# Re-ordering copies, head moves and row transposes in the first attention layer of a four-layer block

## The chip, the core and the metric

The kernel runs on one core of one Trainium2 chip. A core has five engines with instruction streams of their own: TensorE (PE, matmuls), VectorE (DVE), ScalarE (ACT), GpSimd (POOL) and SyncE (SP, which here only issues DMAs). They meet through semaphores. The metric is the device time of one execution in microseconds (us). Before the change it is 1189.37 us, the median of three runs (1189.28 to 1192.3). The profiled execution took 1192.6 us, of which 1190.8 us lie between its first and its last instruction; all times inside the profile count from that first instruction.

## What is computed

Four residual layers, in the order A, B, A, B, on x of 2048 rows and 576 columns in bf16:

```python
x = x + _A_ref(_layernorm(x, axis=-1), A_wqkv, A_wo)
x = x + _B_ref(_layernorm(x, axis=-1), B_w_in, B_w_sp, B_b_sp, B_w_out)
...                                   # the same two once more
# _A_ref: 32 heads of 18 columns; row s attends to rows s, s-2, ..., s-14 that exist
logits = where(mask, einsum(q, kg) * scale, -1e9);  o = einsum(softmax(logits), vg) @ wo
# _B_ref: z = gelu(x @ w_in); z2 = layernorm(second half of z)
# out = (first half of z * (w_sp @ z2 + b_sp)) @ w_out
```

Only the first layer A (`li == 0` in the code) is touched by the change, and the layer B behind it is where its last edits are felt.

## The kernel before

`layer_A` writes out by hand the order of instructions on every engine: inside `manual_schedule`, each engine takes its instructions in the order of the Python calls. So the text of `layer_A` is five in-order queues. The layer has three phases.

**Front (0 to 41 us).** x comes in groups of rows, called tiles, of 128 rows: `x0` holds tiles 0 to 3, `x1` tiles 4 to 7, a spare buffer tiles 8 to 11, and a fourth load tiles 12 to 15. The weights for v, q and k come on the same SP queue between them (`load_wv`, `load_wqk`; here `D` is 576, k is loaded first, then q, then a last strip of k). For a tile i, `S_(i)` takes mean and variance on DVE, `R_` raises to the power -0.5 on POOL, `A_(i)` writes the normalised rows on DVE. They are then transposed into `xnT`, by PE for tiles 0 to 3 (`T_pe`, and a copy by ACT), by SP's transposing DMA for the others (`T_`, line 249). `PG(d, qk, cc)` projects 128 columns of q or k (block d) for 512 rows (cc) with five matmuls of 128x512 (line 402), and copies the result to a staging tile `stg`; two of these tiles, for blocks 3 and 4, are borrowed from the later weight `win2a`. Once all parts of a block of 1024 rows are staged, 18-row slices, one per head, are moved to the tile `QK` by DMAs, spread over the POOL and SP queues by the `queues` argument. `VW(t, hh)` projects v with five matmuls of 128x288 (line 379). `fill_window_rows` writes constant rows of the sliding-window mask into `QK`, half a sequence at a time, in four DVE copies of 128x4096 (line 196); the moves come after the fill of their half.

**Steps (41 to 130 us).** The attention is 38 steps, two for each 112 queries: step s does the logits of step s+1 (`L_mm`, 16 matmuls, line 437), their exponentials (`EXP`, two ACT instructions, line 446), and the product with v of step s (`PV`, 16 matmuls, line 457), which ends with two DVE instructions and, every second step, a transposing DMA into `oT` (line 469). Whatever else is due in a step stands in `table`, filled by `at(step, function)`: the remaining `PG` for rows 1024 to 2047, the `VW`, `WO` (the output projection with residual, line 494), the row norms of the result (`LN_STATS`, `LN_XN`), its store (`XST`), and `LN_T(i)`, the transposing DMA of row tile i back into `xnT` for layer B (line 249 again). `oT`'s and `LN_T`'s transposes, the stores and the loads of the residual all go out on the SP queue.

**Behind it: layer B.** `p1_main(i)` starts at about 134 us. It multiplies row tile i with the second half of `w_in` (line 791), applies gelu on ACT into one of three buffers `zp` (line 805), and takes sums; `p1_norm(i)` normalises `zp` into `Z`, in part on DVE (line 832), in part on POOL (line 834), after a power on POOL (line 822). The bias `bsp` is loaded on POOL's queue into the memory of the four `ln_xn` buffers; so that load stands behind the transposes of the last row tiles, which read these buffers, and in POOL's order it stands ahead of the first power of layer B.

Of the kernel before, what the change touches and what calls it, by code (L numbers as in the profile page):

```python
# [18 lines left out]
P = 128  # L19
D = 576  # L20
# [6 lines left out]
PADL = HALO  # L27
# [35 lines left out]
class K:  # L63
# [51 lines left out]
    def build_window_rows(self, c, R):  # L115

        nc = self.nc
        self.pat = self.consts.tile([P, 2, 272], bf16, name="win_pat")
        self.patpad = self.consts.tile([P, PADL], bf16, name="win_patpad")
        n = c.tile([P, 3], i32, name="win_n")
        g = c.tile([P, 3], i32, name="win_g")
        bits = c.tile([P, 5, 3], i32, name="win_bits")
        vf = c.tile([P, 5, 3], f32, name="win_vf")
        uu = c.tile([P, 4, 2], f32, name="win_uu")
        half = WB / 2  # L130
        nc.gpsimd.iota(n[:], pattern=[[1, 3]], base=15, channel_multiplier=1)
        nc.gpsimd.memset(R[:, 0, 0:8, :], half)
        nc.gpsimd.affine_select(out=R[:, 0, 0:8, :], in_=R[:, 0, 0:8, :], compare_op=ALU.is_ge, fill=-half,
                                base=1, pattern=[[2, 8], [-1, 16]], channel_multiplier=0)
        nc.gpsimd.memset(R[:, 1, 0:8, :], 0.0)
        for off in (2, 3):
            nc.gpsimd.affine_select(out=R[:, 1, 0:8, :], in_=R[:, 1, 0:8, :], compare_op=ALU.not_equal, fill=-1.0,
                                    base=-off, pattern=[[-2, 8], [1, 16]], channel_multiplier=0)
        nc.gpsimd.memset(R[:, 1, 7, 0:2], 1.0)
        for a, v in ((0, half), (1, 1.0)):  # L140
            row = R[:, a, 12, :].rearrange("p (f e) -> p f e", e=2)
            nc.gpsimd.memset(row[:, :, 0:1], v)
            nc.gpsimd.memset(row[:, :, 1:2], -v)
        nc.gpsimd.memset(R[:, 0, 13, :], -2.5 * WB)
        nc.gpsimd.memset(R[:, 1, 13, :], 1.0)
        one = self.dram.tile([2, MR, 256], bf16, name="win_period")
        for xb in self.xn_bufs:
            nc.gpsimd.memset(xb[:, D:640], 0.0)

        def part0():  # L150
            nc.vector.tensor_scalar(out=n[:], in0=n[:], scalar1=15, scalar2=None, op0=ALU.bitwise_and)
            nc.vector.tensor_scalar(out=g[:], in0=n[:], scalar1=1, scalar2=None, op0=ALU.logical_shift_right)
            nc.vector.tensor_tensor(out=g[:], in0=g[:], in1=n[:], op=ALU.bitwise_xor)
            for i in range(4):
                nc.vector.tensor_scalar(out=bits[:, i, :], in0=g[:], scalar1=i, scalar2=1,
                                        op0=ALU.logical_shift_right, op1=ALU.bitwise_and)
            nc.vector.tensor_scalar(out=bits[:, 4, :], in0=n[:], scalar1=1, scalar2=None, op0=ALU.bitwise_and)

        def pads():
            nc.gpsimd.memset(self.pat[:], 0.0)  # L160
            nc.gpsimd.memset(self.patpad[:], 0.0)
            for j in range(4):
                nc.gpsimd.affine_select(out=self.patpad[:], in_=self.patpad[:], compare_op=ALU.not_equal, fill=1.0,
                                        base=-32 * j - 31, pattern=[[0, PADL]], channel_multiplier=1)

        def part1(eng):
            nc.vector.tensor_scalar(out=vf[:], in0=bits[:], scalar1=-2.0, scalar2=1.0, op0=ALU.mult, op1=ALU.add)
            nc.vector.tensor_scalar_mul(out=R[:, :, 0:8, :], in0=R[:, :, 0:8, :], scalar1=vf[:, 4, 1:2])
            nc.vector.tensor_tensor(out=uu[:], in0=vf[:, 0:4, 0:2], in1=vf[:, 0:4, 1:3], op=ALU.add)
            nc.vector.tensor_scalar_mul(out=R[:, 0, 8:12, :], in0=vf[:, 0:4, 1:2].to_broadcast([P, 4, 16]), scalar1=half)  # L170
            nc.vector.tensor_scalar_mul(out=R[:, 1, 8:12, 0:2], in0=uu[:, :, 0:1].to_broadcast([P, 4, 2]), scalar1=0.5)
            nc.vector.tensor_scalar_mul(out=R[:, 1, 8:12, 2:16], in0=uu[:, :, 1:2].to_broadcast([P, 4, 14]), scalar1=0.5)
            self.dma(one[:].rearrange("a r (p f) -> p (a r) f", f=16), R[0:16].rearrange("p a r f -> p (a r) f"), eng=eng)

        def load(eng):
            for j in range(4):
                self.dma(self.pat[32 * j + DH:32 * j + 32, :, 0:256], one[:].rearrange("a r x -> r a x"), eng=eng)
        self.load_pat = load
        return part0, pads, part1

    def make_ident(self):
        nc = self.nc
# [1 line left out]
        nc.gpsimd.affine_select(out=self.ident[:], in_=self.ident[:], compare_op=ALU.not_equal, fill=1.0,  # L184
                                base=0, pattern=[[-1, P]], channel_multiplier=1)

    def fill_window_rows(self, QK, half):
        nc, n = self.nc, self.cfg.S // 2
        if half == 0:
            nc.vector.tensor_copy(out=self.pat[:, :, 256:272], in_=self.pat[:, :, 0:16])  # L190
            nc.vector.tensor_copy(out=QK[:, 0, :, 0:PADL], in_=self.pat[:, 0, None, 0:PADL].to_broadcast([P, 8, PADL]))
            nc.vector.tensor_copy(out=QK[:, 1, :, 0:PADL], in_=self.patpad[:, None, :].to_broadcast([P, 8, PADL]))
        c0 = PADL + half * n
        for g0 in (0, 4):
            for a in range(2):
                nc.vector.tensor_copy(out=QK[:, a, g0:g0 + 4, c0:c0 + n].rearrange("p g (k x) -> p g k x", x=256),
                                      in_=self.pat[:, a, None, None, PADL:PADL + 256].to_broadcast([P, 4, n // 256, 256]))

    def H_tile(self, name):
        return self.ps.tile([P, 2, 512], f32, name=name, tag="H", bufs=2)  # L200
# [82 lines left out]
        nc.vector.memset(R["wv"][64:128, 4, :], 0.0)  # L283
        nc.vector.memset(R["wo"][64:128, 4, :], 0.0)

    def load_wqk(self, eng):

        R = self.right
        for c0, n, w0 in ((D, 512, D + 64), (0, D, 0), (D + 512, 64, D)):
            self.dma(R["wqk"][:, :, w0:w0 + n], self.A_wqkv[0:512, c0:c0 + n].rearrange("(c p) n -> p c n", p=P), eng=eng)  # L290
            self.dma(R["wqk4"][:64, w0:w0 + n], self.A_wqkv[512:576, c0:c0 + n], eng=eng)

# [29 lines left out]
    def layer_A(self, li):  # L322
        nc, tc, cfg = self.nc, self.tc, self.cfg
# [190 lines left out]
            self.ln_T(tails.pop(i)["xn"], i * P, P)  # L514

        q2 = (nc.gpsimd, nc.sync, nc.gpsimd)


        if li == 0:
# [10 lines left out]
            x_load(x0[:, 1:2, :], 1, 1, nc.scalar)  # L530
            x_load(x0[:, 2:4, :], 2, 2, nc.sync)
            self.load_wv(nc.sync, 2)
            x_load(x1[:, 0:4, :], 4, 4, nc.sync)
            self.load_wqk(nc.sync)
            x_load(spare, 8, 4, nc.sync)
            exp_table()
            self.zero_right()
# [46 lines left out]
            R_(1, 1)  # L584
            A_(0)
            T_pe(0)
            S_(2)
            A_(1)
            T_pe(1)
            VW(0, 0, False)  # L590
            VW(0, 1, False)
            VW(1, 0, False)
            S_(3)
            R_(2, 2)
            rows[1]()
            setup_bufs(nc.gpsimd)
            rows[2](nc.gpsimd)
            A_(2, 3)
            T_pe(2)
            T_pe(3)  # L600
            VW(1, 1, False)
            x_load(sb.tile([P, 4, D], bf16, name="x_in3", tag="x_in", bufs=2)[:], 12, 4, nc.sync)
            S_(4, 5)
# [19 lines left out]
            order = [(d, 0) for d in range(4)] + [(d, 1) for d in range(4)] + [(4, 0), (4, 1)]  # L623
            for k_, (d, cc) in enumerate(order):
                for qk in ((1, 0) if d < 4 else (0,)):
                    PG(d, qk, cc, False, (nc.gpsimd, nc.sync) if d in (0, 4) else q2)
                if k_ == 3:
                    VW(3, 0, False)
                    VW(3, 1, False)
                if k_ == 5:  # L630
                    R_(12, 4)
                    A_(12, 13, 14, 15)
# [15 lines left out]
            nvw0, nvw = 0, 4  # L648
        for t in range(nvw0, nvw - (1 if li == 0 else 0)):
            for hh in range(2):  # L650
                VW(t, hh, li == 0)

        pieces = []

# [8 lines left out]
        def at(s, f, *a):  # L663
            table.setdefault(s, []).append((f, a))
        pgs = [(d, qk, cc) for d, cc in ((0, 2), (1, 2), (2, 2), (0, 3), (1, 3), (2, 3), (3, 2), (3, 3), (4, 2), (4, 3))
               for qk in ((1, 0) if d < 4 else (0,))]
        PG_END = 14
        pre, pgs = pgs[:6], pgs[6:]
        for k_, (d, qk, cc) in enumerate(pgs):
            at(1 + k_ if li == 0 else (k_ * PG_END) // len(pgs), PG, d, qk, cc, True)  # L670
        for t in range(nvw, NT):
            for hh in range(2):
                if li == 0 and t == nvw:
                    at(13 * hh, VW, t, hh, True)
                else:
                    at(2 * t - 2 + hh, VW, t, hh, 2 * t - 2 + hh >= PG_END and hh == 0)
        for i in range(NS):
# [6 lines left out]
            at(s + 2, LN_XN, i)  # L684
            at(s + 2, XST, i)
            if i < NS - 1:
                at(max(s + 4, 24 + (5 * i) // 4) if li == 0 else s + 4, LN_T, i)
        if li == 0:
            at(0, self.load_wo, nc.sync)
            for f in reversed(self.load_win2a(nc.gpsimd)):  # L690
                at(0, f)
# [5 lines left out]
        for k_, (d, qk, cc) in enumerate(pre):  # L697
            if k_ == (2 if li == 0 else 0):
                L_mm(0)
                EXP(0)  # L700
            PG(d, qk, cc, li > 0 or k_ < 4, q2)
            if li == 0 and k_ == 3:
                self.fill_window_rows(QK, 1)
        if li == 0:
            VW(nvw - 1, 0, False)
            VW(nvw - 1, 1, False)
# [346 lines left out]
```

The softmax here doesn't subtract the row's maximum and nothing guards it: scores larger than these inputs give would overflow.

## Time and profile before

| | us |
|---|---|
| device time, median of three | 1189.37 |
| span of the profiled execution | 1190.8 |
| PE busy | 1180.2 (99%) |
| DVE busy | 547.4 (46%) |
| ACT busy | 376.6 (32%) |
| POOL busy | 281.5 (24%) |
| first layer A, up to the last output projection | about 0 to 135 |

A PE that is busy for 99% of the span leaves 10.6 us of visible idle time. To find what an edit in layer A can be worth one looks for PE's idle stretches inside the first 160 us, and for what ended each. A row of the timeline reads: start, duration, engine (SPq is SyncE's own queue, which only issues), source line, operation, output<-input, and in brackets the engine's idle time ahead of it with what ended it. A DMA has three times: when its queue issued it, how long the issue took, and when its data landed; only the last lets a waiting instruction go on. In a table of waits the numbers are the sum in us, how often, and the longest.

### The profile page before, as it was taken

What the parts mean: (1) busy time and instruction counts of PE and PEld (TensorE: products, weight loads), DVE (VectorE), ACT (ScalarE), POOL (GpSimd) and SP (SyncE); (2) the same over time, 40 slices, a digit from 0 to 9 for tenths busy, and PEclk for the clock granted to TensorE, in tenths of its full rate; (3) what the DMA queues carried; (4) which work ended last, traced back from release to release, by engine and by line L of the source; (5) the groups of instructions that cost most, each with busy time, mean ns of one, the idle gap of its engine ahead of it and who ended that gap; (6) DMA issues with size and microseconds to landing.
All of it is one profiled execution on the core that took longest, in us unless ns stands there. A gap on an engine that the chain in (4) does not pass through costs nothing.

```text
span 1190.8 us, 20761 instructions
## 1 busy us (share of the span) xinstructions
PE 1180.2 (99%) x8554; PEld 620.6 (52%) x8554; DVE 547.4 (46%) x1206; ACT 376.6 (32%) x593; POOL 281.5 (24%) x383
## 2 busy tenths in 40 slices
PE   8999999999999999999999999999999999999998
PEld 5567544444444444457755775444444444444677
DVE  8688587333233233245556786753233233233311
ACT  5578677210110110202156786760110110111000
POOL 4768685000000000001153877530000000000000
PEclk9999999999999999999999999999999999999999
DMA  8989992000000000049645999900000000000332
GB/s 195 200 163 199 181 224 65 23 4 9 12 12 12 12 1 11 12 139 291 169 98 117 203 227 196 202 14 9 12 12 1 12 12 12 12 1 28 125 105 73
DMA packets 178104, 101.21 MB, mean 85 GB/s; under 512 B 134336, under 2 KB 159360, under 8 KB 178009
## 3 DMA queue, kind: packets, MB, share of 16 engines
q1 hardware_dynamic: 165144, 78.13, 30.6%
q0 software_dynamic: 6512, 16.00, 5.4%
q10 hardware_dynamic: 6352, 5.75, 1.6%
q8 instruction: 67, 1.10, 0.4%
q14 instruction: 29, 0.23, 0.1%
HBM read 42.39 MB, written 16.53 MB: 49 GB/s over the span
## 4 chain that ended last, share of the span: by engine, by line
PE 94%; DMA 3%; POOL 1%; ACT 0%; issue 0%; SPq 0%; DVE 0%; ACTq 0%; DVEq 0%
PE pg L887 42%; PE pz L869 12%; PE po L941 12%; PE pz L791 11%; PE pp L402 5%; PE pw L494 3%; PE O_ps L457 3%; PE pv L379 3%; PE L_ps L437 2%; DMA oT<-o_t 2%; PE pzs L791 1%; DMA QK<-win2a 1%; POOL QK L77 1%; DMA wqk_sb<-in_A_wqkv_dram 1%; ACT P_sb L446 0%
## 5 line engine op out<-in xcount | busy, mean ns | idle before, releaser
L887 PE MATMUL pg<-Wq,Z 128*128 128x512 bf16 x2304 | 502.8, 379 | 0.0
L887 PEld LDWEIGHTS <-Z 128*128 128x128 bf16 x2304 | 225.3, 98 | 272.0
L891 DVE TENSOR_TENSOR g_tmp<-pg,ln_xn 128x512 f32<-128x512 f32 x144 | 99.6, 692 | 429.2 <-PE pg L887 429.2
L881 ACT ACTIVATE z1T<-pz 128x1024 bf16<-128x1024 f32 x72 | 73.7, 1024 | 513.8 <-PE pz L869 513.6
L77 POOL DMA_DIRECT2D wout<-in_B_w_out_dram x4 | 4.3, 1064 | 604.6 <-PE pg L887 604.6
L941 PE MATMUL po<-wout,Z 128*128 128x288 bf16 x1152 | 141.4, 286 | 0.0
L446 ACT ACTIVATE P_sb<-L_ps 128x896 bf16<-128x896 f32 (+1 forms) x152 | 126.7, 887 | 41.2 <-PE L_ps L437 40.6
L869 PE MATMUL pz<-xnT,w 128*128 128x512 bf16 (+1 forms) x640 | 136.0, 380 | 0.0
L941 PEld LDWEIGHTS <-Z 128*128 128x128 bf16 x1152 | 112.7, 98 | 28.8
L791 PEld LDWEIGHTS <-xnT 128*128 128x128 bf16 (+1 forms) x800 | 66.2, 97 | 81.0 <-issue 23.7
L791 PE MATMUL pz<-win2a,xnT 128*128 128x512 bf16 x384 | 104.8, 380 | 0.0
L892 DVE TENSOR_TENSOR Z<-g_tmp,z1T 128x512 bf16<-128x512 f32 x144 | 99.6, 692 | 9.7
L869 PEld LDWEIGHTS <-w 128*128 128x128 bf16 (+1 forms) x640 | 51.1, 97 | 80.0 <-issue 27.1
L402 PE MATMUL pp<-xnT,wqk_sb 128*128 128x512 bf16 x360 | 83.8, 382 | 0.5 <-DMA wqk_sb<-in_A_wqkv_dram 0.5
L805 ACT ACTIVATE zp<-pz 128x1024 bf16<-128x1024 f32 x64 | 65.5, 1024 | 36.6 <-PE pz L791 32.8
L951 DVE TENSOR_TENSOR x_new<-po,xo 128x288 f32<-128x288 f32 (+1 forms) x64 | 28.8, 455 | 87.6 <-PE po L941 83.5
L791 PE MATMUL pz<-win2b,xnT 128*128 128x512 bf16 (+1 forms) x256 | 65.7, 380 | 0.0
L807 DVE CUSTOM_DVE_ANT_0 Z<-zp 128x1536 bf16<-128x1536 bf16 x32 | 56.6, 1769 | 13.1 <-ACT zp L805 13.0
L77 POOL DMA_DIRECT2D QK<-stg x81 | 50.7, 631 | 36.3 <-DVE stg L371 21.0
L379 PE MATMUL pv<-wv_sb,xnT 128*128 128x288 bf16 (+1 forms) x380 | 55.8, 285 | 0.0
L242 POOL TENSOR_SCALAR ln_xn<-x_new,ln_mv,ln_rstd 128x576 bf16<-128x576 f32 x23 | 52.8, 2294 | 2.0
L402 PEld LDWEIGHTS <-wqk_sb 128*128 128x128 bf16 x360 | 33.2, 98 | 37.2 <-DMA wqk_sb<-in_A_wqkv_dram 1.0
(114 smaller groups left out, 916.9 us busy)
## 6 DMA issues: line engine op xcount, KB each, us to landing
xres<-x_new SPq DMA_DIRECT2D x48, 288.0 KB
xo<-xres SPq DMA_DIRECT2D x32, 288.0 KB
wout<-in_B_w_out_dram POOLq DMA_DIRECT2D x4, 1296.0 KB, 8.5
xo<-xres SPq DMA_DIRECT2D x8, 576.0 KB
w<-in_B_w_in_dram SPq DMA_DIRECT2D x16, 256.0 KB
QK<-stg POOLq DMA_DIRECT2D x53, 72.0 KB, 4.4
QK<-stg SPq DMA_DIRECT2D x41, 72.0 KB
xo<-in_A_x_dram SPq DMA_DIRECT2D x8, 288.0 KB
```

The lines of the kernel that those rows point to most:

```text
L77: return eng.dma_start(out=out, in_=in_)
L379: nc.tensor.matmul(pv[:nk, 0:288], lhsT=self.xnT[:, c, QT * t:QT * t + nk], rhs=wv_sb[:, c, hh * 288:(hh + 1) * 288], start=(c == 0), stop ...
L402: nc.tensor.matmul(pp[:, :], lhsT=w, rhs=self.xnT[:, c, PADL + cc * 512:PADL + (cc + 1) * 512], start=(c == 0), stop=(c == 4))
L446: nc.scalar.activation(out=P_bufs[(2 * s + jp) % 4][:nk, :, :, 0:nq], in_=Lv[:nk, :, :, 0:nq], func=ACT.Exp, scale=scale)
L791: nc.tensor.matmul(pzvs[ci][:, sub * 512:sub * 512 + w], lhsT=self.xnT[r0:r1, c, PADL + i * P:PADL + (i + 1) * P], rhs=win2(c)[r0:r1, c0 + ...
L805: nc.scalar.activation(out=zp[:, c0:c0 + cn], in_=pzvs[ci][:, 0:cn], func=ACT.Gelu_apprx_tanh, accum_out=sums[:, ci:ci + 1])
L869: nc.tensor.matmul(pz1s[q // 2][:, q % 2, :], lhsT=w1[r0:r1, c, sub * P:(sub + 1) * P], rhs=self.xnT[r0:r1, c, PADL + q * 512:PADL + (q + ...
L881: nc.scalar.activation(out=z1T[:, q2 * 512:(q2 + 2) * 512], in_=pz1s[q2 // 2][:, :, :].rearrange("p a b -> p (a b)"), func=ACT.Gelu_apprx_ ...
L887: nc.tensor.matmul(pg[:, :], lhsT=Z[:, jj, i, sub * P:(sub + 1) * P], rhs=Wq[q][:, i, :], start=(i == 0), stop=(i == NS - 1))
L891: nc.vector.tensor_tensor(out=tmp[:], in0=pg[:, :], in1=bsp[:, qs], op=ALU.add)
L892: nc.vector.tensor_tensor(out=uT(jj)[:, sub, qs], in0=tmp[:], in1=z1Ts[jj, sub][:, qs], op=ALU.mult)
L941: nc.tensor.matmul(acc[hh], lhsT=uT(j // 2)[:, j % 2, i * P:(i + 1) * P], rhs=wouts[j // NJH][:, j % NJH, hh * 288:(hh + 1) * 288], start= ...
```

## The change

It has six parts, all in the first attention layer:

1. **Loads.** `load_wqk` is cut in pieces: k and the first 256 columns of q (`q0`) are now issued before x tiles 4 to 7, the rest of q (`q1`) and the last strip of k behind them.
2. **First row norms.** The small DVE instructions that build the mask pattern (`part1`, now without its store) move ahead of the norm of tile 1; the statistics of tiles 2 and 3 follow that norm, and each of these two tiles has its own power. The pattern's memsets and its store on POOL come after tile 3.
3. **Mask copies.** The fill of the second half, four copies in one go before the steps, becomes one copy at the end of each of steps 0 to 3.
4. **Last head moves.** The eight moves of block 4 of the first half go to SP seven times out of eight, where they alternated between POOL and SP.
5. **Order of projections.** `VW(9, 1)` moves from step 13 to step 1; twelve `PG` that stood one in each of steps 1 to 12 now stand two in step 2 and one in each of steps 3 to 12. `VW` of t = 4 and 5 are copied out by ACT where DVE did it.
6. **Late row transposes.** `LN_T` of row tiles 4 to 11 moves from steps 29, 30, 31, 32, 34, 35, 36, 37 to steps 34, 34, 35, 35, 36, 36, 37, 37; those of tiles 12 to 14 from steps 39, 40, 41 to steps 36, 38, 41.

The purpose is to have PE wait less for data: for q's weights, for the second step's head moves, and for the `oT` transposes at the end. Between the two programs nothing else changes: PE has the same number of instructions in both.

```diff
-        def part1(eng):
+        def part1():
...
+        def store(eng):
             self.dma(one[:].rearrange("a r (p f) -> p (a r) f", f=16), R[0:16].rearrange("p a r f -> p (a r) f"), eng=eng)
...
-    def fill_window_rows(self, QK, half):
+    def fill_window_rows(self, QK, half, parts=((0, 0), (0, 1), (4, 0), (4, 1))):
...
-    def load_wqk(self, eng):
+    def load_wqk(self, eng, names=("k", "q", "k1")):
...
-        for c0, n, w0 in ((D, 512, D + 64), (0, D, 0), (D + 512, 64, D)):
+        parts = dict(k=(D, 512, D + 64), q=(0, D, 0), q0=(0, 256, 0), q1=(256, D - 256, 256), k1=(D + 512, 64, D))
+        for c0, n, w0 in (parts[k_] for k_ in names):
...
+        q7 = (nc.sync,) * 7 + (nc.gpsimd,)
...
             self.load_wv(nc.sync, 2)
+            self.load_wqk(nc.sync, ("k", "q0"))
             x_load(x1[:, 0:4, :], 4, 4, nc.sync)
-            self.load_wqk(nc.sync)
+            self.load_wqk(nc.sync, ("q1", "k1"))
...
             A_(0)
             T_pe(0)
-            S_(2)
+            rows[2]()
             A_(1)
             T_pe(1)
+            S_(2)
+            R_(2, 1)
             VW(0, 0, False)
             VW(0, 1, False)
             VW(1, 0, False)
             S_(3)
-            R_(2, 2)
+            R_(3, 1)
+            A_(2)
+            T_pe(2)
+            A_(3)
+            T_pe(3)
             rows[1]()
             setup_bufs(nc.gpsimd)
-            rows[2](nc.gpsimd)
-            A_(2, 3)
-            T_pe(2)
-            T_pe(3)
+            rows[3](nc.gpsimd)
...
-                    PG(d, qk, cc, False, (nc.gpsimd, nc.sync) if d in (0, 4) else q2)
+                    PG(d, qk, cc, False, (nc.gpsimd, nc.sync) if d == 0 else q2 if d < 4 else q7)
...
-                VW(t, hh, li == 0)
+                VW(t, hh, li == 0 and t > 5)
...
-            at(1 + k_ if li == 0 else (k_ * PG_END) // len(pgs), PG, d, qk, cc, True)
+            at(2 + (11 * k_) // 12 if li == 0 else (k_ * PG_END) // len(pgs), PG, d, qk, cc, True)
...
-                    at(13 * hh, VW, t, hh, True)
+                    at(hh, VW, t, hh, True)
...
-                at(max(s + 4, 24 + (5 * i) // 4) if li == 0 else s + 4, LN_T, i)
+                at(s + 4 if li > 0 or i > 11 else 24 + i if i < 4 else 34 + (i - 4) // 2, LN_T, i)
...
+            for k_, part in enumerate(((0, 0), (0, 1), (4, 0), (4, 1))):
+                at(k_, self.fill_window_rows, QK, 1, (part,))
...
-            if li == 0 and k_ == 3:
-                self.fill_window_rows(QK, 1)
```

More of the change, by code (lines that the diff above doesn't have):

```diff
@@ L178, in build_window_rows @@
         self.load_pat = load
-        return part0, pads, part1
+        return part0, pads, part1, store
     def make_ident(self):
@@ L193, in fill_window_rows @@
         c0 = PADL + half * n
[L194 to L197, printed above, removed]
+        for g0, a in parts:
+            nc.vector.tensor_copy(out=QK[:, a, g0:g0 + 4, c0:c0 + n].rearrange("p g (k x) -> p g k x", x=256),
+                                  in_=self.pat[:, a, None, None, PADL:PADL + 256].to_broadcast([P, 4, n // 256, 256]))
     def H_tile(self, name):
```

## The prediction, on record before the run

> **What bounds the kernel now.** I read the page's first part, then PE's table of waits for 5 to 160 us, then the timelines of PE, DVE, POOL, ACT and SP around each wait, with the landing times that the trace's semaphore updates give.
>
> ```profile
> PE 1180.2 (99%) x8554; PEld 620.6 (52%) x8554; DVE 547.4 (46%) x1206; ACT 376.6 (32%) x593; POOL 281.5 (24%) x383
> ...
> PE pw L494 <- DMA oT<-o_t: 1.8, 2, 1.2
> PE pt L574 <- DVE ln_xn L567: 1.2, 2, 0.8
> PE L_ps L437 <- ACT P_sb L446: 0.9, 3, 0.3
> PE L_ps L437 <- DMA QK<-win2a: 0.7, 1, 0.7
> PE pp L402 <- DMA wqk_sb<-in_A_wqkv_dram: 0.5, 1, 0.5
> ```
>
> PE sets the end, and only 10.6 us of it are free to win; the waits that the change aims at are 1.8 + 0.7 + 0.5 = 3.0 us, with the slow starts around them about 4. One more cost hides in a busy PE. The windows view (stretch, length, busy time of PE, PEld, DVE, ACT, POOL, granted clock, DMA share, GB/s):
>
> ```profile
> 51.00:53.20 2.20, 2.20 (x13) 0.54 (x13) 0.71 (x2) 1.33 (x2) 0.05 (x1) 0.50 1.06 337
> ```
>
> For 3.4 us after the wait for head moves PE's clock is 0.50, and the projection there takes 2.29 us instead of 1.24. Then the rows that decide what replaces these waits (timelines):
>
> ```profile
> 10.84 0.82 DVE L554 BATCH_NORM_STATS2 ln_st<-x_in 128x6 f32<-128x288 bf16 x2 [0.36 <-DMA x_in<-in_A_x_dram]
> 14.34 6.26 SPq L249 DMA_TRANSPOSE xnT<-ln_xn  x4
> 23.26 10.95 PE L402 MATMUL pp<-xnT,wqk_sb 128*128 128x512 bf16 x50
> 44.65 1.34 POOL L77 DMA_DIRECT2D QK<-win2a  x1 [0.57 <-DMA QK<-win2a]
> 126.80 1.19 SPq L469 DMA_TRANSPOSE oT<-o_t  x1
> 143.79 1.28 SPq L249 DMA_TRANSPOSE xnT<-ln_xn  x1
> 147.00 0.64 POOL L77 DMA_DIRECT2D ln_xn<-in_B_b_sp_dram  x1 [5.42 <-DMA xnT<-ln_xn]
> 151.22 1.02 ACT L805 ACTIVATE zp<-pz 128x1024 bf16<-128x1024 f32 x1 [1.02 <-POOL Z L834]
> ```
>
> DVE already waits for x tiles 4 to 7 at 10.84. The last `oT` transpose goes out at 126.80 although its rows were written at 123.04: SP was behind. And the last row transpose (143.79, landed 146.45) holds POOL until 147.00, so that ACT's first gelu of tile 3 starts 1.02 late, with 0.55 us to spare for PE (its PSUM is free at 152.24, PE wants it at 152.79).
>
> **The skill.** The Trainium skill, "TensorE: Matmul & The Clock Gate", Part 1, says that too little PE activity in a free-running window of about 3.4 us halves the clock; the trace agrees (one period of 3.413 us at 0.50). "DMA: Bandwidth & Descriptors", Issuing engines are not separate DMA queues, says that all queues share the same 16 DMA engines, so another queue saves issue time alone; the trace agrees that issue is not all: SP's moves land 5.5 us after issue at 41 us against 2.9 at 28.
>
> **The change, part by part.**
>
> Row norms: tile 1 gains about 0.2 us, which PE spends waiting for tile 2 anyway. Tile 3 has a power of its own (0.58 us on POOL, at 4.81) between statistics and norm, so its transposes start at about 10.97 where tile 2 and 3 together ended at 10.83: +0.45. The k projection starts at 13.13 instead of 12.68; q follows at 14.22, since q0 has landed by then, instead of 14.47: -0.25.
>
> Loads: k and q0 pass x tiles 4 to 7. In this trace k took 1.67 us of the queue (10.82 to 12.49), its tail 0.26, and half of q's 1.68 is 0.84: x lands 2.8 us later, or 2.5 by the typical DMA engine; I take 2.7, so 13.5. From there DVE's chain keeps its lengths, but the wait of 0.83 for tile 8 (16.66) vanishes: norms of tiles 6 and 7 at +5.87, transpose of tile 7 issued at +7.6, landed 2.7 later: 23.8, where it was 22.06. PE wants it, for rows 512 to 1023, at 23.26 - 0.25 = 23.0. New wait 0.8; sum so far +0.55 (0 to +1.2). Behind DVE's chain also stand the transposes of tiles 8 to 11 (+1.8 us), the first half's fill and with it the moves (POOL 27.34 to 28.4, SP 28.38 to 30.1).
>
> Last head moves: three moves leave POOL, where each took 0.55 of issue and the last waited for an earlier landing (44.65, landed 48.81), and cost SP 0.72 each. SP's 19 moves then run from 30.1 to about 45.5, the last landing 4.5 to 5 us behind its issue: 49.6 (48.5 to 50.7), against 48.81. Queued behind them on SP are the transposes of tiles 12 to 15, 3.9 us later (landed 50.02 before, about 54 after); `PG` of rows 1536 to 2047 needs them, and its step 2 comes at about 54. POOL turns earlier to `win2a` loads, which share the DMA engines. Step 0 thus starts +0.8 later (-1.3 to +1.9), the front's +0.55 included.
>
> Mask copies: 4 x 1.22 us of DVE. Before, they lay under PE's wait (44.68 to 49.32). In steps 0 to 3 DVE has 10.7 us of work against 9 of PE; it falls behind by two PSUM tiles of the four that projections and `PV` share. I cost it at nothing: PE's next tile is free each time. ACT's copies of `VW` 4 and 5 save 0.1.
>
> Order of projections: a step with a `PG` takes about 2.07 us of PE (L4 to L9, 55.25 to 65.73); one with a `VW` only the 1.85 that two exponentials need (1.73 and the hand-over). Steps 1 and 2: 2 x 2.07 = 4.14 before, 1.85 + 3.16 after, less 0.2 of hand-over: +0.65. Step 13 loses its `VW`: 2.07 to 1.85, -0.22. Sum +0.43.
>
> Late transposes: the four that stood ahead leave SP free at 118.4 and 123.1, when `oT` is ready. It lands by about 122 and 127; PE wants it at 124.6 and 129.4. Both waits go: 0.75 + 1.40 = 2.15 with their slow starts. But SP then has twelve row transposes behind the last `oT` instead of eight: 17.0 us from 126.80 to 143.79 becomes 17.0 + 4 x 1.29 = 22.2, less up to 1.7 in issues that were stretched, from 123.15: the last goes out at 144 to 145.3, lands at 146.7 to 148, and PE's fifth tile starts 5.8 later, as before: 152.5 to 153.8. With the gain PE would want 150.64. So this wait takes back nearly all; if stores keep no SP time over 0.6 each it is 151.5. I take 151.9, -0.9 (-2.1 to +1.0).
>
> Sum: +0.8 + 0.43 - 0.9 = +0.33, so 1189.7.
>
> **Rivals.** (a) Waits move and grow: x lands at 13.8, the head moves at 50.7 (+1.9), the last transposes late (+0.5), the steps +0.43, and the longer waits bring one more slow window of 3.4 us at half clock, +1.7: +4.5, 1193.9. For it: x's wait at 10.84, SP issuing without a pause from 28.38 to 48.37, 0.55 us of slack at 152.24. Against: PE's clock stayed at 1.00 after the 1.23 us wait at 131. (b) Waits go: row tiles arrive in time, the moves land before PE asks (0.25 + 1.15 saved), the slow window goes with that wait (1.35), the end keeps 2.15, the steps cost 0.43: -4.5, 1184.9. For it: three moves fewer on POOL, whose last one ended the wait, and 3.7 us of SP lateness removed. Against: the 2.7 us of x, which nothing in DVE's chain makes up, and POOL's wait for the last transpose.
>
> **How the numbers follow.** Forecast 0.5, rival (a) 0.26, rival (b) 0.24. 0.3% is 3.6 us, so the forecast counts as no change, (a) as slower, (b) as faster. Range 1184.7 to 1195.0: it takes in (b), and (a) with a second slow window's part.
>
> **What would show it.** A DVE wait of about 3 us for x near 13.5; a PE wait for `xnT` near 23 to 24; the logits of step 1 at about 49.6 behind `QK`; no PE wait for `oT`; a PE wait near 150 with POOL's power behind the last row transpose. I am wrong if x lands by 12, if the last head move lands by 47.5, or if POOL's bias load waits no longer than before.

## The result, and the profile after

The kernel after takes 1199.02 us, the median of six runs (1196.1 to 1203.65); before, beside it, 1191.01 us (1189.28 to 1195.27). The ratio is 1.0067, with a 95% interval of 1.0039 to 1.0094: 8 us slower, where 1189.7 us (0.33 above the 1189.37 of the first three runs) was forecast in a range up to 1195.0. The profiled execution spans 1196.2 us, 5.4 us more than before.

The page's first part, after:

```profile
PE 1180.9 (99%) x8554; PEld 621.1 (52%) x8554; DVE 545.6 (46%) x1203; ACT 377.4 (32%) x597; POOL 278.8 (23%) x381
```

PE's table of waits from 5 to 160 us, after (sum in us, how often, longest):

```profile
PE pp L404 <- DMA xnT<-ln_xn: 2.7, 1, 2.7
PE pz L798 <- ACT zp L812: 2.0, 2, 1.8
PE pt L578 <- DVE ln_xn L571: 1.9, 4, 0.7
PE L_ps L439 <- ACT P_sb L448: 1.6, 5, 0.4
PE L_ps L439 <- DMA QK<-win2a: 0.9, 1, 0.9
PE L_ps L439 <- DMA QK<-stg: 0.5, 1, 0.5
```

The waits that the change aimed at, for q's weights (0.5 us) and for `oT` (1.8 us), are gone. The one for head moves has stayed (0.7 us before, 0.9 after), and one of 0.5 us for earlier head moves is new, ahead of it. Two larger ones stand in their place: 2.75 us for row transposes of the front, and 2.0 us in layer B. PE's waits for normalised rows at the start grew from 1.2 to 1.9 us, but the logits of step 0 still start no later. Where the 5.4 us arise is read from the start of the same PE instruction in both timelines:

| PE starts | before | after | difference |
|---|---|---|---|
| logits of step 0 | 41.31 | 41.13 | -0.18 |
| logits of step 1 | 47.28 | 47.85 | +0.57 |
| logits of step 4 | 55.25 | 60.22 | +4.97 |
| logits of step 37 | 128.10 | 132.41 | +4.31 |
| first output projection after the last `oT` | 131.51 | 134.42 | +2.91 |
| third row tile of layer B | 143.35 | 146.59 | +3.24 |
| fifth row tile of layer B | 152.63 | 157.83 | +5.20 |

By the logits of step 4 PE after has also done `VW(9, 1)`, 0.61 us of work that before still has ahead. These logits open step 3, and those of step 1 open step 0. So steps 0 to 2, between these two rows, took 12.37 us instead of 7.97, and cost 12.37 - 7.97 - 0.61 = 3.79 us. The `oT` waits then give 2.15 back, of which 0.7 is lost again in steps 15 to 36 (0.3 of it in longer waits for the exponentials), and layer B takes 0.33 + 1.96. PE's timeline in step 2:

```profile
52.98 0.56 PE L459 MATMUL O_ps<-v_ext,P_sb 128*128 128x19 bf16 x16
56.29 4.00 PE L404 MATMUL pp<-xnT,wqk_sb 128*128 128x512 bf16 x10 [2.75 <-DMA xnT<-ln_xn]
60.22 0.40 PE L439 MATMUL L_ps<-QK 32*128 32x112 bf16 x16
```

The ten matmuls of the two projections wait from 53.54 to 56.29, and then take 4.0 us, where one projection takes 1.17 in each of the next steps, so 2.3 for two. The windows view (stretch, length, busy time of PE, PEld, DVE, ACT, POOL, granted clock, DMA share, GB/s) says why:

```profile
57.50:60.50 3.00, 3.00 (x23) 0.97 (x21) 0.79 (x2) 0.00 (x0) 0.00 (x0) 0.56 0.26 31
```

The clock is halved for one period of 3.41 us from 56.7, right behind the wait; 0.56 is the mean over this window. Before had such a period too, at 50.5, behind its wait for head moves.

Why the transposes are late shows on the queues. SP's timeline, after:

```profile
43.93 1.44 SPq L77 DMA_DIRECT2D QK<-win2a  x2
45.47 5.35 SPq L250 DMA_TRANSPOSE xnT<-ln_xn  x4
50.88 1.28 SPq L77 DMA_DIRECT2D wo_sb<-in_A_wo_dram  x2
```

And POOL's timeline, after:

```profile
44.17 1.68 POOL L77 DMA_DIRECT2D win2a<-in_B_w_in_dram  x3
49.73 2.54 POOL L77 DMA_DIRECT2D win2a<-in_B_w_in_dram  x3 [3.88 <-DMA QK<-win2a]
```

SP issues its last head move at 44.67 and then the transposes of tiles 12 to 15, the last of them at 49.59; before it went out at 45.91. The last head move lands at 49.11. That frees the rest of the `win2a` staging memory, and POOL sends its last three loads into it from 49.73 on. So loads of 864 KB begin at the moment at which the last transpose is issued, and `wo` follows on SP. By the semaphore updates in the trace this transpose lands 6.56 us after its issue, at 56.15; the four of tiles 8 to 11, with no bulk load beside them, took 2.61 to 2.64 each.

The issue of a load alone does not tell the two kernels apart. Before, POOL's first load went out just as close behind the last transpose:

```profile
45.91 1.23 SPq L249 DMA_TRANSPOSE xnT<-ln_xn  x1
45.99 1.17 POOL L77 DMA_DIRECT2D win2a<-in_B_w_in_dram  x1
```

But its 4608-byte packets (the pieces that the DMA engines move) began only at 48.53, when the transpose's own 256-byte packets were ending. After, they ran from 50.99, and from 50.9 to 52.1 the transpose's own nearly stopped.

### The profile page after: what moved, and what is told of

It is laid out like the page before. It is cut to its first block, busy times and chain, and to the rows that moved or that the text cites. A ratio compares the mean times of both kernels' runs of the same rounds, so it can differ in the third digit from the quotient of the medians.

```text
span 1196.2 us, 20767 instructions
## 1 busy us (share of the span) xinstructions
PE 1180.9 (99%) x8554; PEld 621.1 (52%) x8554; DVE 545.6 (46%) x1203; ACT 377.4 (32%) x597; POOL 278.8 (23%) x381
## 4 chain that ended last, share of the span: by engine, by line
PE 94%; DMA 1%; SPq 1%; DVE 1%; ACT 1%; issue 1%; POOL 0%; ACTq 0%; POOLq 0%; DVEq 0%
PE pg L894 42%; PE pz L876 12%; PE po L948 12%; PE pz L798 10%; PE pp L404 6%; PE pw L496 3%; PE pv L381 3%; PE O_ps L459 3%; PE L_ps L439 2%; PE pzs L798 1%; SPq L77 1%; DMA xnT<-ln_xn 1%; ACT P_sb L448 1%; DMA QK<-win2a 0%; DMA xnT<-stg 0%
## 5 line engine op out<-in xcount | busy, mean ns | idle before, releaser
L243 POOL TENSOR_SCALAR ln_xn<-x_new,ln_mv,ln_rstd 128x576 bf16<-128x576 f32 x23 | 52.7, 2291 | 2.0
```

## The experiments

Every kernel is timed against before on the same chip. "Parts" are those of the change.

| kernel | median, us | ratio to before, 95% interval |
|---|---|---|
| after: all six parts | 1199.02 | 1.0067 (1.0039 to 1.0094) |
| e3: part 4 alone | 1195.44 | 1.0033 (1.0021 to 1.0046) |
| e1: all but part 4 | 1196.48 | 1.0042 (1.0026 to 1.0059) |
| e2: all but part 5 | 1200.73 | 1.0071 (1.0049 to 1.0094) |
| e12: part 1 alone | 1194.20 | 1.0020 (1.0011 to 1.0029) |
| e10: parts 1, 2, 3, 5 | 1195.04 | 1.0025 (1.0013 to 1.0037) |
| e15: parts 2, 3, 5 | 1192.93 | 1.0010 (1.0001 to 1.0019) |
| e5: part 6 alone | 1193.48 | 1.0011 (1.0002 to 1.0020) |
| e6: part 6, bias load on SP | 1191.91 | 1.0007 (0.9992 to 1.0023) |
| e7: after, bias load on SP | 1197.35 | 1.0050 (1.0033 to 1.0068) |
| e4: after, `win2a` in steps 5 to 10 | 1202.85 | 1.0097 (1.0077 to 1.0117) |
| e8: after, `wo` in step 4 | 1207.53 | 1.0118 (1.0095 to 1.0141) |
| e9: after, `wo` on POOL | 1201.54 | 1.0077 (1.0056 to 1.0099) |
| e11: e10, `wo` on POOL | 1194.92 | 1.0021 (1.0011 to 1.0031) |
| e13: after, both behind `oT` on SP | 1199.12 | 1.0063 (1.0043 to 1.0084) |
| e14: before, both behind `oT` on SP | 1198.69 | 1.0051 (1.0033 to 1.0068) |
| e16: e15, both behind `oT` on SP | 1198.21 | 1.0043 (1.0029 to 1.0056) |

**Part 4, the head moves, with and without the rest (e3, e1).**

```diff
 # e1, on after
-PG(d, qk, cc, False, (nc.gpsimd, nc.sync) if d == 0 else q2 if d < 4 else q7)
+PG(d, qk, cc, False, (nc.gpsimd, nc.sync) if d in (0, 4) else q2)
 # e3, on before: the other way round, with q7 = (nc.sync,) * 7 + (nc.gpsimd,)
```

> The kernel before with part 4 alone: the last head moves go to SP seven times out of eight. Theory Q: the last transpose of tiles 12 to 15 is issued 2.2 us later, at about 48.1, and lands at 52 to 54.5 instead of 50.02; PE, which asks for it at about 50.9 in step 1, waits 1.5 to 3.5 us; the slow window is there in both. Time 1.5 to 4 us above before. Rival O: nothing waits for xnT, the head moves land a little sooner, and the time is that of before or up to 1 us less.

> The kernel after with part 4 undone: the last head moves alternate between POOL and SP again; all else as after. In the profile of after PE waits 2.75 us at 56.29 for the transposes of tiles 12 to 15 (the last issued at 49.59, landed at 56.15), and then runs 3.4 us at half clock. Theory Q (SP is late because of three more moves in front of these transposes): three moves of 0.75 us less on SP, so the last transpose is issued 2.2 us earlier, at about 47.4, and lands at 51.5 to 53.5; PE's wait is under 0.5 us, the slow window behind it is gone or smaller, and the time falls by 3 to 4.5 us, to about 1195. Rival O (two projections in one step is what costs): time within 1 us of after. Rival C (the six loads of win2a on POOL hold the DMA engines, whatever SP does): the last transpose still lands at 55 or later, and the wait stays over 1.5 us.

Alone on before, part 4 costs 0.33%, 3.9 us. PE's waits in e3:

```profile
PE pp L402 <- issue: 3.4, 1, 3.4
```

The profile names no releaser here, but the last transpose lands at 53.31 and PE goes on at 53.40, in step 1, after 3.37 us; the transpose was issued at 48.38, 2.5 us later than before, and took 4.93 us instead of 4.11. (The longer transfer is within chance: e5 and e6 below, whose front is that of before, show 5.60 and 4.90.) Undone in after (e1), the transpose is issued at 47.26, lands at 52.62, and PE has no wait for it. The median is 2.5 us below that of after, where theory Q had 3 to 4.5, and the two intervals overlap, so in time the gain is not shown. In e1's profile one other wait appeared, 1.33 us for `oT` at 86.50 with 6.8 us of half clock behind it. For the wait theory Q holds; rival C does not hold as stated, because the transpose landed at 52.6.

**The order of projections (e2).**

```diff
-at(2 + (11 * k_) // 12 if li == 0 else ..., PG, d, qk, cc, True)
+at(1 + k_ if li == 0 else ..., PG, d, qk, cc, True)
-at(hh, VW, t, hh, True)
+at(13 * hh, VW, t, hh, True)
-VW(t, hh, li == 0 and t > 5)
+VW(t, hh, li == 0)
```

> The kernel after with part 5 undone: one projection in each of steps 1 to 12, VW(9, 1) in step 13, and VW 4 and 5 copied by DVE. Theory Q: the transposes still land at about 56, and PE asks for them one step sooner, at about 51; its wait grows to 4.5 to 5.5 us, less work is done before it, and the time is 1 to 2 us above after, about 1200.5. Rival O (the order is the cause): no wait over 1 us for xnT, and the time falls by 2.5 to 4 us, to about 1195.5.

PE asks at 52.61 in step 1 and waits 5.37 us until the last transpose has landed at 57.85. So the new order is not the cause of the wait; with it PE asks 0.93 us later (53.54). In time e2 can't be told from after.

**Parts 1, 2, 3 and 5 (e12, e10, e15).** e12 adds part 1 to before; e10 is after with parts 4 and 6 undone, e15 with part 1 undone as well.

```diff
 # e12, on before, with load_wqk as in after (e15 undoes these lines in after)
+self.load_wqk(nc.sync, ("k", "q0"))
 x_load(x1[:, 0:4, :], 4, 4, nc.sync)
-self.load_wqk(nc.sync)
+self.load_wqk(nc.sync, ("q1", "k1"))
```

> The kernel before with part 1 alone: k and the first 256 columns of q are loaded ahead of x tiles 4 to 7. In after these tiles landed at 12.31 instead of 10.82, and the last transpose of tiles 4 to 7 at 22.94 instead of 22.06. Theory F (the prediction's front): q's wait of 0.55 us goes, a wait of 0 to 1 us for xnT comes at 23, SP's first move is issued 0.9 us later; time 0 to 1 us above before. Rival D (the delay runs on through SP's queue to the transposes of tiles 12 to 15, which have 0.9 us to spare at 50.9): PE waits 0.3 to 1.5 us for xnT in step 1, and the time is 1 to 2.5 us above before.

> The kernel after with parts 4 and 6 undone, which leaves the loads, the first row norms, the mask copies and the order of projections. Part 4 alone cost 4.0 us on before, part 6 alone 1.3 us. Theory N (the other parts cost nothing): the time is that of before within 1 us, 1190.5 to 1192.5. Theory R (the order with VW first and the copies in the steps crowd the DMA queues of steps 13 to 17: with part 4 undone PE waited 1.34 us for oT at 86.5 and ran a slow window): such a wait is there again at 80 to 100 us, and the time is 2 to 4 us above before, 1193.5 to 1195.5.

> The kernel after with parts 1, 4 and 6 undone, which leaves the row norms, the mask copies and the order of projections. Parts 1, 2, 3 and 5 together were 3.0 us above before, part 1 alone 2.4. Additive: 0 to 1.2 us above before. Rival R (the order with VW first crowds later steps): 2 us or more above before, with a wait for oT or QK between 55 and 100 us. Rival B (part 1 hid a gain: with the transposes of tiles 12 to 15 early and PE asking for them a step later, the waits of the front go): 1 us or more below before.

Part 1 alone costs 0.20%, 2.4 us: rival D. Two rows of PE's waits in e12:

```profile
PE pp L403 <- DMA xnT<-ln_xn: 2.3, 1, 2.3
PE pw L495 <- DMA oT<-o_t: 2.3, 2, 2.1
```

x lands at 12.37 and the wait for q is gone, and at 23 PE waits only 0.1 us. But the last transpose of tiles 12 to 15 is issued 0.57 us later than before, at 46.48, and lands at 53.27, where PE asked at 50.99. So the loads of the first 15 us are paid for at 51 us, though not by the late issue alone: the transpose also took 6.79 us, where three traces with the front of before have 4.11 to 5.60. The wait for `oT` at 135.31, 2.07 us, is longer than the 1.23 of before as well. Parts 1, 2, 3 and 5 together cost 3.0 us, parts 2, 3 and 5 alone 1.2. The profile of e10 does not have the wait at 80 to 100 us that theory R wanted (it waits 1.3 us for head moves at 48.8 and 1.5 for `oT` at 133.4), so its time came as R said and its reason did not. Within parts 2, 3 and 5 the 1.2 us were not traced further; in e15's profile the last transpose lands at 53.48, and PE waits 0.77 us until 53.61. The profile puts this wait down to a mask copy on DVE (line 197), which ended at 53.61. The row gives busy time and mean ns of all these matmuls, then their idle time and what ended most of it:

```profile
L404 PE MATMUL pp<-xnT,wqk_sb 128*128 128x512 bf16 x341 | 82.5, 384 | 1.8 <-DVE QK L197 0.8
```

In after, e3, e4 and e12 PE went on 0.05 to 0.14 us after the landing, here 0.13, so the transpose explains the wait too; which of the two it was stays open.

**Part 6, and the bias load (e5, e6, e7).**

```diff
 # e5: part 6 alone on before. e6 and e7 add this, in both layers B:
-self.dma(bsp, self.B_b_sp.partition_broadcast(P), eng=nc.gpsimd)
+self.dma(bsp, self.B_b_sp.partition_broadcast(P), eng=nc.sync)
```

> The kernel before with part 6 alone: the transposes of row tiles 4 to 14 of the result go out behind the last oT. The prediction's step, tested by itself. Theory L (it gives at the oT waits and takes at POOL): the two waits for oT (0.59 and 1.23 us, with slow starts 2.15) are gone; the last row transpose is issued 20.5 to 22.2 us behind the one of oT(16), as in after, where it was 21.2, so at about 144 to 145 and landed at 146.5 to 148; with PE 2 us earlier than before the fifth tile of layer B then waits 0.5 to 1.9 us for ACT, and the time is 0 to 2 us below before. Rival G (the waits go and nothing comes back): 2 us or more below before, no wait of PE on the fifth tile. Rival H (the late transposes are the main loss of the change): 1 us or more above before.

> The kernel before with part 6, and with the load of layer B's bias issued on the sync queue behind the loads of Wq, in both layers B, instead of on POOL's queue ahead of POOL's first power. Theory L: nothing holds POOL's first power any more, so the wait of PE on the fifth tile of layer B is gone and the 2 us of the oT waits are kept: 1 to 2.5 us below the same kernel with the load on POOL where that one has such a wait, about 1189 where before is 1191. Rival S (the last row transpose itself is what layer B waits for): the wait stays where it was, and the time with it.

> The kernel after with the load of layer B's bias issued on the sync queue behind the loads of Wq, in both layers B, instead of on POOL ahead of its first power. In after PE waits 1.80 us at 157.83 and 0.16 at 146.59 for ACT, which waits for POOL's first Z. Theory L (POOL is held by the bias load until the last row transpose has landed, at 151.8): POOL's first power comes at about 147.3, the wait of 1.8 us is gone, and the time falls by 1.5 to 2.3 us, to about 1197. Rival S (layer B waits for the row transposes themselves, or ACT is behind by itself): a wait of over 1 us stays in the first six tiles, and the time stays within 0.7 us of after.

Part 6 alone costs 0.11%, 1.3 us (0.2 to 2.4). Theory L had 0 to 2 us below before; the time fits rival H's "1 us or more above", though part 6 is not the main loss (part 4 alone costs 3.9). Two rows of e5's table of waits:

```profile
PE pz L791 <- ACT zp L805: 2.5, 2, 1.5
PE pw L494 <- DMA oT<-o_t: 0.5, 1, 0.5
```

The `oT` waits at the end are gone (the 0.5 us left are at 88). But layer B waits twice: 1.46 us on the fifth row tile, as theory L said, and 1.00 us on the third, which nobody had said. DVE's timeline of after at the first sum of squares of layer B:

```profile
144.69 1.76 DVE L814 CUSTOM_DVE_ANT_0 Z<-zp 128x1536 bf16<-128x1536 bf16 x1 [4.74 <-DMA xnT<-stg]
```

The same instruction in DVE's timeline of e5:

```profile
139.45 1.76 DVE L807 CUSTOM_DVE_ANT_0 Z<-zp 128x1536 bf16<-128x1536 bf16 x1 [5.68 <-DMA xnT<-stg]
```

This sum writes its unused squares into free memory of `Z`, and the trace has it released by the transposes that read `stg`, the rows of tiles 4 to 12. With four more of them behind the last `oT`, the last lands at 138.69 in e5 and 144.42 in after, and DVE and ACT wait for it. Before, it landed at 138.73, but there layer B was 3.3 us later than in e5 (ACT's first gelu at 136.35 for 133.08), and the same instruction started at 139.72 and was released by ACT's gelu. No run gave the squares other memory, so this cause is read from the trace; in e5 the sum starts 0.76 us after the landing (0.27 in after), and what filled that gap is not known. What the fifth tile waits for shows in POOL's timeline of after:

```profile
152.45 0.64 POOL L77 DMA_DIRECT2D ln_xn<-in_B_b_sp_dram  x1 [8.36 <-DMA xnT<-ln_xn]
```

POOL stands still until the last row transpose has landed (151.80), issues the bias load, and only then takes its first power.

With the bias load on SP (e6) the wait on the fifth tile is gone and the one on the third is left (0.91 us); e6 can't be told from before. In e7 the fifth tile's wait of 1.8 us is gone too, but in its profile the third tile's has grown to 2.75, because the last `stg` transpose landed at 148.76; the time, 1197.35 us, can't be told from after. So the POOL wait is shown, and so is that it was not alone.

**Which loads delay the transpose (e4, e8, e9, e11).**

```diff
 # e4, on after
-at(0, f)              # six loads of win2a, POOL
+at(5 + k_, f)         # k_ counts the loads
 # e8, on after
-at(0, self.load_wo, nc.sync)
+at(4, self.load_wo, nc.sync)
 # e9, on after, and e11, on e10: behind the loads of win2a
-at(0, self.load_wo, nc.sync)
+at(0, self.load_wo, nc.gpsimd)
```

> The kernel after with the six loads of win2a issued in steps 5 to 10, one each, instead of all in step 0; PE, DVE, ACT and SP keep their order. Theory C (the loads share the DMA engines with the transposes and add to their latency: 6.56 us for the last one, where an undisturbed one takes 2.6): the last transpose lands within 3 us of its issue at about 49.6, so by 52.6, before PE asks at 53.5; no wait, no slow window, and the time falls by 4 us, to about 1195. Theory Q alone, without C: it still lands at 55 or later, the wait stays over 1.5 us, and the time within 1.5 us of after.

> The kernel after with the two loads of wo moved from step 0 to step 4 on the sync queue, where they stood directly behind the transposes of tiles 12 to 15. In after the last of these transposes has its last 256-byte packets at about 53.1, but its semaphore moves only at 54.0 to 56.15, with the packets of wo and of win2a running in between. Theory W (the wo load, next in the same queue, delays the end of the last transpose): it lands by 53.5, PE's wait of 2.75 us falls under 0.5 us, the slow window behind it goes, and the time falls by 3 to 4.5 us. Rival C (the win2a loads of POOL do it): it lands at 54.5 or later, the wait stays over 1 us, and the time falls by less than 2 us.

> The kernel after with the two loads of wo issued on POOL's queue behind the six of win2a, in step 0, instead of on the sync queue directly behind the transposes of tiles 12 to 15. With wo in step 4 the last transpose landed 2.67 us after its issue instead of 6.56, but wo itself came 4.4 us late at 73. Theory W (what follows directly on the same queue delays the end of a transpose): it lands by 52.6, the wait of 2.75 us for xnT is under 0.5 us, wo is in time, and the time falls by 3 to 4.5 us, to about 1195. Rival C (the bytes of wo and win2a in the shared DMA engines do it, on whichever queue): it lands at 54.5 or later, and the time falls by less than 1.5 us.

> The kernel after with parts 4 and 6 undone and the loads of wo on POOL's queue behind those of win2a. Theory W: the last transpose of tiles 12 to 15 lands within 3.2 us of its issue at about 47.3, so by 50.5; PE has no wait for it; the front is then 1 to 2 us better than with wo on the sync queue, and the time is at or below before: 1189 to 1191.5. Rival C: no difference to the same kernel with wo on the sync queue beyond 0.7 us.

The last transpose of tiles 12 to 15 in each profile, with PE's request for it:

| kernel | issued | landed | took | PE asks | PE waits |
|---|---|---|---|---|---|
| before | 45.91 | 50.02 | 4.11 | | 0 |
| after | 49.59 | 56.15 | 6.56 | 53.54 | 2.75 |
| e5: front as before | 44.79 | 50.39 | 5.60 | 50.19 | 0.34 |
| e6: front as before | 45.60 | 50.49 | 4.90 | 49.69 | 0.94 |
| e7: front as after | 50.16 | 57.53 | 7.37 | 54.23 | 3.44 |
| e4: no `win2a` beside it | 49.95 | 54.50 | 4.55 | 52.83 | 1.81 |
| e8: no `wo` behind it | 49.23 | 51.90 | 2.67 | | 0 |
| e9: `wo` on POOL | 51.37 | 57.40 | 6.03 | 56.28 | 1.26 |
| e13: neither | 48.71 | 53.26 | 4.54 | 51.85 | 1.54 |
| e14: before, neither | 44.82 | 48.36 | 3.54 | | 0 |
| e16: e15, neither | 46.35 | 49.20 | 2.85 | | 0 |

Each row is one profile, and e5, e6 and e7 show how far chance goes: with an unchanged front the time from issue to landing differs by up to 1.5 us. In e4 and e8 one of the two kinds of load is moved away and the transpose gets faster by more than that, though in e4 it stays above the 3 us that theory C wanted; in e9 `wo` goes to another queue, and it is hardly faster. In e8 the three late `win2a` loads go out at 50.25, 1 us behind the transpose; in e9 at 51.39, within 0.02 us of it, and their 4608-byte packets run from 52.7 to 53.9 while its own do not. So which bulk loads move beside it decides more than the queue does. That fits the sentence of the Trainium skill that the prediction used ("DMA: Bandwidth & Descriptors", Issuing engines are not separate DMA queues: all queues share 16 DMA engines), and e11 agrees, with the same time as e10 (its transpose took 6.78 us, e10's 5.50).

But against before on its own chip e8 is slower than after by 0.51%, about 6 us, and e4 by 0.30%, 3.6 us. The load put off comes late itself, or into the head moves of steps 6 to 16. Two rows of e8's waits:

```profile
PE pw L496 <- DMA wo_sb<-in_A_wo_dram: 5.2, 2, 4.4
PE L_ps L439 <- DMA QK<-win2a: 1.8, 2, 1.5
```

In e4 it is `oT`, for which PE waits 5.3 us in two waits (85.92 and 94.80).

**Both loads behind the first oT (e13, e14, e16).**

```diff
-at(0, self.load_wo, nc.sync)
-for f in reversed(self.load_win2a(nc.gpsimd)):
-    at(0, f)
+for f in reversed(self.load_win2a(nc.sync)):
+    at(1, f)
+at(1, self.load_wo, nc.sync)
```

> The kernel after, all six parts, with the eight loads of win2a and wo issued on the sync queue in step 1, behind the first oT transpose, so that no bulk load stands before, beside or directly behind the transposes of tiles 12 to 15. In after the last of them took 6.56 us from issue to landing; with wo away it took 2.67, with win2a away 4.55, with wo on POOL's queue 6.03. Theory C (bulk loads in flight beside it make the difference, whichever they are and on whichever queue): it takes 2.6 to 3.2 us, lands at 52 to 52.8, PE's wait of 2.75 us at 56.29 and the slow window behind it are gone, and the time falls by 3 to 4.5 us, to about 1195, if the loads collide with nothing later. Rival P (the transposes are late by their issue alone): it lands at 54.5 or later, and the time falls by less than 1 us.

> The kernel before with the same edit alone: win2a and wo on the sync queue in step 1, behind the first oT transpose. Theory C: the last transpose of tiles 12 to 15, issued at 45.9, lands by 49.2 instead of 50.02, the last head moves land 0.3 to 1 us earlier than 48.81, and PE's wait for them (1.26 us with slow starts) shrinks to under 0.7; time 0.5 to 2 us below before. Rival D (the bytes are only moved into the crowd of head moves at 56 to 90 us): a wait of over 0.8 us for oT or QK appears at 55 to 100 us, and the time is that of before or above.

> Parts 2, 3 and 5 alone, with win2a and wo on the sync queue in step 1 behind the first oT transpose. Theory C and B together: the transposes of tiles 12 to 15 and the head moves meet no bulk load, PE asks for the transposes only in step 2, no wait of over 0.6 us between 20 and 60 us and no slow window there; time 1 to 3 us below before. Rival D (bytes moved into a crowd): a wait for oT or QK at 55 to 100 us of over 0.8 us; time of before or above.

On before and on e15 the transpose takes 3.54 and 2.85 us and lands in time. Yet both kernels are slower than without the edit: rival D. The first row of e14's waits:

```profile
PE pw L494 <- DMA oT<-o_t: 3.8, 2, 3.1
```

The second `oT` transpose was issued at 61.01 and landed at 69.10, 8.1 us later, behind the eight loads and the head moves; in e16 it took 9.1 us, and PE waited 3.5 us at 71.15. In e13 nothing of the kind came, but its own transpose still took 4.54 us with only an `oT` transpose issued behind it (51.08), neither theory C's 2.6 to 3.2 nor rival P's landing at 54.5. Fifteen of the transpose's sixteen semaphore updates had come after 2.75 us; the last came 1.8 us later. PE waited 1.54 us, two half-clock periods came with it, and the waits in layer B took 2.6 us; the time is that of after. None of these edits made a version that is faster than before.

## Why the prediction was wrong

**The step that failed.** In "Last head moves" the prediction named the queue and the reader: the transposes of tiles 12 to 15 would be 3.9 us later, would land at "about 54", and `PG` "comes at about 54". It then put nothing for it into the sum, neither the wait nor a range for it. The issue was right, 3.68 us later (49.59 for 45.91). Two sizes were not. The transpose was taken to last 4.11 us as before, and took 6.56 (7.37 in e7, with the same front): bulk loads moved beside it, and it was shorter where one kind of them was put off (e4, e8), but why they held it up more than before is not settled. And PE asks at 53.54. So a gap of zero was 2.75 us, and with the slow clock behind it steps 0 to 2 cost 3.79 us where 0.43 stood for the order of projections. e3 and e12 show the same wait made by part 4 and by part 1, each alone (3.37 and 2.33 us), and e1 shows it gone when part 4 is undone.

**The front.** x was put at 13.5 and landed at 12.31; q's wait went; PE's new wait at 23, put at 0.8, did not come. The front to step 0 gained 0.18 instead of losing 0.55. The head moves were put at 49.6 and landed at 49.11; +0.8 for the start of step 0 was +0.57 where the logits of step 1 start and +0.30 where the last of them starts, which waits for the head moves (49.16 for 48.86).

**Mask copies.** The prediction had them "under PE's wait" before; in the stretch that it gives, 44.68 to 49.32, PE waited 0.69 us. After shows no wait for them, e15's profile puts 0.77 us down to one, which is open (above), and that they cost nothing was not tested apart from parts 2 and 5.

**Late transposes.** The mechanism was right: both `oT` waits went, the last row transpose was issued 21.2 us behind the last `oT` transpose (put at 20.5 to 22.2), and POOL, held by the bias load until 152.45, made PE wait on the fifth tile. The term was mis-sized: -0.9 was forecast and +1.3 measured alone. In the trace of after this end costs 0.33 + 1.96 = 2.29 us against 2.15 won. The prediction had one wait there, and there are two: the sum of squares behind the `stg` transposes was not seen, and e6 shows it without the bias load.

**The sum.** By single runs part 4 costs 3.9 us, part 1 2.4, part 6 1.3, parts 2, 3 and 5 1.2: 8.8 us, against 8.0 for all. Each has an interval of about 1 us or more to either side, so the runs allow that the parts simply add up, and do not show it. Rival (a), "waits move and grow", had the direction and 0.26 of the chance; its 4.5 us left out the one wait that grew most.

**The clock.** Medians differ by more than the two profiled spans (8.0 against 5.4). Part of this can be seen: among 38 executions of before on one chip, those with a mean clock of 1.000 took 1189.0 to 1193.3 us, and those at 0.996 and 0.997 took 1192.9 to 1196.5; the six of after lie at 0.994 to 0.999. A period of 3.41 us at half clock is 0.0014 of the mean and 1.7 us of matmuls.

## What to carry to other kernels

A DMA put on an in-order queue is to be charged to everything behind it: list each transfer that stands behind, when its reader asks for it, and the margin; where that margin is near zero in a forecast, the wait belongs in the sum with a size of its own. A transfer's time from issue to landing is not a constant of its kind, so ask which bulk loads will be moving at that moment. And when loads are moved out of one crowd, find the next one before moving them.

## What the runs showed of the hardware

The same transpose, 128 rows of 640 columns, took 2.6 us from issue to landing with no bulk load in flight at 23 to 31 us, 2.85 and 3.54 us where the loads were moved away on e15 and before (e16, e14), 4.54 in e13 with the last update late, and 4.1 (before) to 7.4 us (e7, e15) with bulk loads about it. Only e8's took 2.67 us there: the packets of its loads began when the transpose's own were over. In e4 its last 256-byte packets ended at about 52.0, and its semaphore moved at 54.35 to 54.50, with packets of the `wo` load, one of them 1.1 us long, in between. What holds the end back is not settled: in e9, where the next DMA on its own queue went out 3.8 us behind it, it took 6.0 us. One candidate was never tried: a packet of 16384 bytes that the trace calls "instruction" ran from 52.04 to 53.20 in e4 and from 51.21 to 52.13 in e13, each ahead of the late updates, and there is one of about 1 us in after, e2, e7 and e9 too. It can't be the whole cause, since e15, with 7.36 us, has none. Half-clock periods came in multiples of 3.41 us, most of them in or behind a wait of PE, and their number does not follow the length of the wait: one behind 0.69 us in before and with 2.75 in after, two with 1.33 in e1, 3.37 in e3 and 2.33 in e12, three with 4.27 in e4, none with 0.94 in e6. In e7 three began at 51.63, ahead of its wait of 3.44 us and behind three of 0.3 to 0.4; and e5 has one at 687.6, in a layer that no edit touched, behind waits of 0.36 and 0.13, where before has the same waits and no such period.
